# Scaling the values instead of the keys, and summing the first states on TensorE, in a retention layer with a feed-forward layer

## The chip, the cores and the metric

The kernel runs on one core of one Trainium2 chip. The metric is the device time of one execution in microseconds; the median of three runs counts. A second figure is the span of one profiled execution, from its first instruction to its last, which is a little shorter than the device time of that execution.

## The reference

Eight batches of eight heads, 576 positions of 64 numbers each, go through retention: attention without a softmax, in which the score of a query and a key falls by a factor gamma of the head with each step between them. The result, 4608 tokens of 512 numbers, goes through a feed-forward layer of 2048 with an ELU between.

```python
scores = q @ k.T / sqrt(64)                 # per batch and head
gamma  = 1 - 2 ** (-5 - head)
ret    = where(i >= j, scores * gamma ** (i - j), 0)
x      = (ret @ v)                          # heads side by side: 4608 x 512
h      = x @ w_in                           # 512 x 2048
out    = where(h > 0, h, exp(min(h, 0)) - 1) @ w_out    # 2048 x 512
```

## The kernel before

**The decay as two factors.** gamma^(i-j) is gamma^i times gamma^-j. The kernel keeps two small tables, `gq` (with the scale) and `gk`, and multiplies each query by its entry of `gq` and each key by its entry of `gk` while casting to bfloat16. The mask then only has to zero the upper triangle.

**Chunks and states.** A sequence is cut into blocks of 256 positions (`T` = 0, 1) and a tail of 64. Within a block, positions attend to each other by scores and mask; what lies before them comes in by a state, the sum of key times value over all earlier positions, 64 by 64 for each head. The first three batches are cut finer, into *units*: one batch, one block, four of the eight heads (`w` = 0, 1). Units 0 and 1 are the first block of batch 0, units 2 and 3 its second block, units 4 and 5 the first block of batch 1, and so on to 11. A unit has two chunks `c`, which lie on partitions 0 to 63 and 64 to 127. Units 0 to 5 are called *early* (`EARLY`): their scores and states are groups of their own on TensorE (`early`); later units and items are joined in pairs (`stretch`).

**A unit's way.** SyncE loads its queries, keys and values as float32 (tiles `r`; for the first two blocks the values come after the keys, `VLATE`). In `prepare_unit` two multiplies (even and odd positions, `e`) make bfloat16 queries and two make keys, in a tile `st`; one cast makes the values, tile `vn`. Queries and keys are transposed, by TensorE and a copy (tile `T`) up to unit 4 and by a DMA from unit 5 on (`PE_TURN`). TensorE then makes the scores, VectorE masks them into `pt` (L913), TensorE makes the unit's state (`do_state`, matmuls `vn,st`), and at last its output: the state before it times the queries (`T,s`) and the masked scores times the values (`pt,vn`). The output is cast to `xt`, the input of the feed-forward layer.

**The states' sums.** `do_state` makes one sum for each chunk, from 64 partitions each; the eight matmuls of chunk 0 and the eight of chunk 1 are interleaved and lie on different rows of the array. `after_state_unit` copies the first sum from PSUM into a float32 tile `mid` or adds it to the last one there, and casts each running sum into a bfloat16 tile `s` that TensorE can use.

**The feed-forward layer.** `ffn1` makes 512 columns by a group of matmuls (tile `f` in PSUM; 8 matmuls for a block of 256 tokens), ScalarE the exponential `e`, ScalarE or VectorE a relu or `em`, VectorE the ELU `g`. `ffn2` multiplies `g` by `w_out`, and the result leaves through `ot`. The weights are loaded by nine DMAs that GpSimd issues (`wi0` to `wi4` for w_in, `wo0` to `wo3` for w_out), in the queue of GpSimd's own instructions.

**The order.** Every step is an operation of a plan (`Plan.run`), with a cost for each engine that may do it, a rank and, for some, an earliest time (`AT`, `RANKS`). The plan is run with these costs before anything is issued; it chooses engine, order and buffer, and each engine then carries out its own list in that order, waiting where an input is not there. Tiles come from fixed numbers of slots (`SLOTS`; "f" are the eight PSUM banks). A group that needs several banks reserves them through `gate`, which lets it wait while at least `SURE` second-layer groups are ready. Where the plan sees TensorE idle in the first 50 us, it puts in filler matmuls on zeros (L1219, or `zero` at L275), as many as the gap it computed has room for. `HOLD` keeps the loads of unit 4 back until w_out's second piece has landed (L399). All matmuls have line L275 in the profile, transposes L579.

Of the kernel before, what the change touches and what calls it, by code (L numbers as in the profile page):

```python
# [12 lines left out]
BF16 = mybir.dt.bfloat16  # L13
I32 = mybir.dt.int32
AF = mybir.ActivationFunctionType
ALU = mybir.AluOpType
# [19 lines left out]
class Plan:  # L36
# [170 lines left out]
JOINT = True  # L207
BD_ACT = 0.6
TWO, STEP = 2, 4
WI, WI1, LD = 1.3, 1.65, 0.84  # L210
MOST, MOSTU = 4, 3
BD_POOL = 0.46
# [10 lines left out]
APART = (4, 5)  # L223
HOLD = {"ldq4": "wo1"}
VLATE = (0, 1)
AT = {"wi0": 8.5, "wi1": 9.1, "wi2": 8.7, "wi3": 11.8, "wi4": 15.0, "wo0": 15.9, "wo1": 18.0, "wo2": 18.9, "wo3": 25.0}
RANKS = {}
FREE = ("f", "e", "em", "g", "ot")
SURE = 3
ATT = ((0, 0), (0, 1), (1, 0), (1, 1), (2, 0), (2, 1), (3, 0), (3, 1), (4, 0), (4, 1), "X",  # L230
       (5, 0), (5, 1), (6, 0), (6, 1), (7, 0), (7, 1), "Y")
FFN = tuple(((b, T),) for b in range(7) for T in range(2)) + (("X", "Y"), ((7, 0), (7, 1)))
# [1 line left out]
W_OUT = ((0, 1), (1, 2), (2, 3), (3, 4))  # L234

SLOTS = {
    "f": 8, "r": 8, "st": 4, "kv": 3, "T": 4, "pt": 2, "vn": 5, "s": 6, "mid": 6,
    "xt": 3, "g": 33, "e": 4, "em": 4, "ot": 6, "S": 5, "bd": 8, "be": 8,
}

# [2 lines left out]
def kernel(  # L243
# [92 lines left out]
    def T(cls, key, shape, dt):  # L336
        return (cls, key, shape, dt)
# [198 lines left out]
    def prepare_unit(u):  # L536
        n = u.n
        key, vkey, tkey = ("qkn", n), ("vn", n), ("qkT", n)
        hs, begun, cq = slice(4 * u.w, 4 * u.w + 4), {}, {}
        for i in range(2):  # L540
            for e in range(2):
                g = (gq, gk)[i][:, 2 * u.T + e, hs].rearrange("p (x y) -> p x y", y=2)
                g = g.unsqueeze(3).to_broadcast([P, 2, 2, D])

                def emit(op, i=i, e=e, g=g):
                    raw = tiles["rqk", n].rearrange("p (h e) d -> p h e d", e=2)[:, 4 * i : 4 * i + 4, e]
                    pin(alu[op.eng].tensor_tensor(tiles[key][:, i, e].rearrange("p (y x) d -> p x y d", y=2),  # L547
                                                  raw.rearrange("p (x y) d -> p x y d", y=2), g, ALU.mult))

                kw, use = taking(begun, "st", key, [P, 2, 2, 4, D])  # L550
                cq[i, e] = add(f"c{'qk'[i]}{e}{n}", {"POOL": 0.62, "DVE": 0.5} if n < 4 else {"POOL": 0.64, "DVE": (0.6, 1.5)},
                               [u.ld["qk"[i]]], emit, u.rank, use=[("rqk", n), *use], **kw)
                begun.setdefault(key, cq[i, e])
        u.ck = [cq[1, 0], cq[1, 1]]

        def emit_v(op):
            pin(copy[op.eng](tiles[vkey], tiles["rv", u.it.n].rearrange("p (h e) d -> p h e d", e=2)[:, hs]))  # L557

        u.laid = [add(f"cv{n}", {"ACT": 0.62, "POOL": 0.65, "DVE": (0.42, 0.3)} if n < 4 else {"POOL": 0.65, "ACT": (0.62, 1.0)},
                      [u.ld["v"]], emit_v, u.rank, take=[T("vn", vkey, [P, 4, 2, D], BF16)], use=[("rv", u.it.n)])]  # L560
        u.cv = u.laid[0]

        def flat():
            return tiles[key].rearrange("p i e h d -> p (i e h d)")

        if n >= PE_TURN:
            def emit_t(op):
                pin(nc.sync.dma_start_transpose(tiles[tkey], flat()))

            u.turned = [add(f"tr{n}", {"SP": 1.23}, list(cq.values()), emit_t, -1, take=[T("T", tkey, [P, 8, P], BF16)],  # L570
                            use=[key], dma=(1.7, 64))]
            return
        u.turned = []
        for i in range(2):
            bkey = ("T", n, i)

            def emit_t(op, i=i, bkey=bkey):
                for j in range(4):
                    pin(nc.tensor.transpose(tiles[bkey][:, j], flat()[:, (4 * i + j) * P : (4 * i + j + 1) * P], ident))  # L579

            t = add(f"T{n}_{i}", {"PE": 0.35}, [cq[i, 0], cq[i, 1]], emit_t, u.rank - 4, take=[T("f", bkey, [P, 4, P], BF16)],
                    use=[key])

            def emit_c(op, i=i, bkey=bkey):
                pin(copy[op.eng](tiles[tkey][:, 4 * i : 4 * i + 4], tiles[bkey]))

            kw, use = taking(begun, "T", tkey, [P, 8, P])
            u.turned.append(add(f"cp{n}_{i}", {"DVE": 0.42, "ACT": 0.59}, [t], emit_c, u.rank - 4, use=[bkey, *use],
                                banks=[(bkey, 0)], **kw))
            begun.setdefault(tkey, u.turned[0])  # L590
# [180 lines left out]
    def do_state(it, tkey, off, st):  # L771
        if it.unit:
            kn, vn = tiles["qkn", it.n], tiles["vn", it.n]
            for b in range(2):
                for e in range(2):
                    for c in range(2):
                        for d in range(2):
                            to = (tkey, c if off == 0 else 1 - c)
                            st.put(c, d, to, tiles[to][rows(d), off + b * D : off + (b + 1) * D],
                                   kn[rows(c), 1, e, 2 * b + d], vn[rows(c), 2 * d + b, e])  # L780
            return
        kv = tiles["kv", it.n].rearrange("p m (h d) -> p m h d", h=H)
        for s in range(2):
            for z in range(2):
                for b in range(2):
                    for par in range(2):
                        for d in range(2):
                            st.put(par, d, (tkey, par), quad((tkey, par), s, 2 * b + z, rows(d)),
                                   kv[rows(par), KS[s], 4 * b + 2 * z + d], kv[rows(par), VS[s], 4 * z + 2 * d + b])
# [43 lines left out]
    def after_state_unit(u, st, tkey, off):  # L833
        for c in range(2):
            cc = 2 * u.T + c + 1
            bank, skey = (tkey, c if off == 0 else 1 - c), ("us", u.b, cc, u.w)
            prev = total.get((u.b, u.w))

            def st_ap(bank=bank):
                return tiles[bank][:, off : off + P].rearrange("p (h d) -> p h d", h=2)  # L840
# [24 lines left out]
            def emit_b(op, skey=skey, bkey=bkey):  # L865
                pin(copy[op.eng](tiles[bkey], tiles[skey]))

            bd_op.setdefault(bkey, []).append(
                add(f"ub{u.n}_{c}", {"POOL": UB_POOL, "ACT": (0.3, 0.3), "DVE": (0.2, 0.4 if u.early else 1.5)}, [s_op], emit_b,
                    u.rank + 3, take=[T("s", bkey, [P, 2, D], BF16)], use=[skey]))  # L870

    def after_state(it, st, tkey, off):
        if it.unit:
# [123 lines left out]
    def stretch(prev, it):  # L997
# [4 lines left out]
            use += inter_uses(prev)  # L1002
            cost += cost_of(prev, "iv") + (0.23 if it is None else 0)
        if it is not None:
            deps += [*it.turned, *([it.cv] if it.unit else [] if it.tail else it.laid)]
            use += [turned_of(it)] + ([] if not it.unit and it.tail else inputs_of(it))
            cost += cost_of(it, "s" if not it.unit and it.tail else "st")
        state = it is not None and (it.unit or not it.tail)
# [16 lines left out]
    def early(it):  # L1025
# [3 lines left out]
        mask_step(it, sc)  # L1029
        if it.unit or not it.tail:  # L1030
            tkey = ("t", it)
            st = add(f"st{name}", {"PE": cost_of(it, "t") + 0.17}, [*it.ck, it.cv] if it.unit else it.laid,
                     lambda op: alone(do_state, it, tkey, 0), it.rank + 1, use=inputs_of(it))
            reserve(st, pair_of(tkey))
            after_state(it, st, tkey, 0)
# [222 lines left out]
```

## Time and profile before

| | us |
|---|---|
| median of 3 runs | 299.97 |
| lowest and highest | 299.42, 300.76 |
| profiled execution, device time | 299.04 |
| its span | 297.3 |
| TensorE busy | 291.7 (98%) |
| VectorE busy | 201.7 (68%) |
| ScalarE busy | 160.3 (54%) |
| GpSimd busy | 118.6 (40%) |

In the profile PE is TensorE, PEld its loads of weights, DVE VectorE, ACT ScalarE, POOL GpSimd and SP SyncE. A row of a timeline gives the start in us, the length, the engine, the line, the operation, what it writes and reads, the shape and the count; in square brackets the idle time before it and what ended it. The clock that the profile grants TensorE is at its full value throughout. What is said of TensorE's being busy has to be read with care: filler matmuls count as busy too.

### The profile page before, as it was taken

To read this page: it belongs to the slowest core of one execution; us is meant where nothing else is said; L and a number is where in the kernel's file an instruction comes from. 1 tells how busy PE (TensorE), PEld (TensorE's weight loads), DVE (VectorE), ACT (ScalarE), POOL (GpSimd) and SP (SyncE) were. 2 spreads that over 40 slices of the span, in tenths; PEclk is the share of its full clock that TensorE was granted. 3 is DMA by queue.
4 is the path that set the end of the run, shared out by engine and by line. 5 is a ranking of instruction groups with operands and counts; after the bars stand their busy time and mean duration, and the time that the engine had idled before them with its cause. 6 is when DMAs were issued, how large, how long until landed. Compare 5 with 4: busy or idle time off the path is not lost.

```text
span 297.3 us, 9176 instructions
## 1 busy us (share of the span) xinstructions
PE 291.7 (98%) x3819; PEld 188.5 (63%) x3819; DVE 201.7 (68%) x385; ACT 160.3 (54%) x298; POOL 118.6 (40%) x193
## 2 busy tenths in 40 slices
PE   7999999999999999999999999999999999999995
PEld 4778556776665766677667676767666444444444
DVE  4979644878765867677787777767877567766500
ACT  3578514876633755466556466464565548644311
POOL 5980288394727361557447356370820000000000
PEclk9999999999999999999999999999999999999999
DMA  7999999999989994699989599987451100011221
GB/s 201 289 207 207 274 264 271 296 232 253 204 210 202 265 194 119 162 252 200 277 207 214 130 227 212 255 151 174 125 109 37 37 35 35 0 37 35 49 96 71
DMA packets 124554, 50.67 MB, mean 170 GB/s; under 512 B 84448, under 2 KB 120032, under 8 KB 124512
## 3 DMA queue, kind: packets, MB, share of 16 engines
q1 hardware_dynamic: 119760, 45.89, 66.3%
q0 software_dynamic: 4752, 4.19, 8.8%
q8 instruction: 30, 0.49, 0.7%
q14 instruction: 12, 0.10, 0.1%
HBM read 36.70 MB, written 9.44 MB: 155 GB/s over the span
## 4 chain that ended last, share of the span: by engine, by line
PE 94%; POOL 2%; DMA 2%; SPq 1%; issue 0%; ACT 0%; ACTq 0%
PE f L275 94%; DMA r<-in_v_dram 2%; POOL w_in_sb L479 1%; SPq L388 1%; POOL vn L557 0%; PE f L579 0%; POOL st L547 0%; ACT ot L1127 0%; PE f L1219 0%; ACTq L1127 0%
## 5 line engine op out<-in xcount | busy, mean ns | idle before, releaser
L275 PE MATMUL f<-w_out_sb,g 128*128 128x512 bf16 (+1 forms) x592 | 141.6, 374 | 0.0
L275 PE MATMUL f<-xt,w_in_sb 128*128 128x256 bf16 (+1 forms) x1024 | 141.1, 286 | 0.0
L1066 ACT ACTIVATE e<-f 128x512 f32<-128x512 f32 x144 | 85.5, 598 | 79.4 <-PE f L275 76.9
L275 PEld LDWEIGHTS <-w_in_sb 128*128 128x128 bf16 x1024 | 99.3, 98 | 38.6
L275 PEld LDWEIGHTS <-g 128*128 128x128 bf16 x592 | 56.6, 98 | 49.7
L1080 DVE TENSOR_SCALAR em<-e 128x512 bf16<-128x512 f32 x87 | 43.2, 496 | 40.6 <-ACT e L1066 40.4
L1090 DVE SCALAR_TENSOR_TENSOR g<-f,em 128x512 bf16<-128x512 f32 x87 | 59.3, 689 | 5.9
L1088 DVE SCALAR_TENSOR_TENSOR g<-e,f 128x512 bf16<-128x512 f32 x57 | 38.1, 683 | 11.3 <-ACT f L1076 10.2
L1127 ACT COPY ot<-f 128x512 f32<-128x512 f32 (+1 forms) x37 | 21.2, 574 | 22.5 <-PE f L275 22.1
L604 POOL CAST kv<-r 128x512 bf16<-128x512 f32 x24 | 14.3, 619 | 47.2 <-PE f L275 37.6
L624 POOL TENSOR_TENSOR kv<-r,gq 128x512 bf16<-128x512 f32 x24 | 25.7, 1091 | 15.4 <-DMA r<-in_q_dram 15.4
L1076 ACT ACTIVATE f<-f 128x512 f32<-128x512 f32 x52 | 30.7, 597 | 0.0
L949 ACT CAST xt<-f 128x512 bf16<-128x512 f32 (+1 forms) x39 | 21.5, 605 | 13.5 <-PE f L275 13.3
L624 POOL TENSOR_TENSOR kv<-r,gk 128x512 bf16<-128x512 f32 x24 | 25.3, 1056 | 3.9 <-DMA r<-in_k_dram 3.9
L913 DVE TENSOR_TENSOR pt<-f,mask_u 128x512 bf16<-128x512 f32 x24 | 15.4, 683 | 3.2 <-PE f L275 3.1
L917 DVE TENSOR_TENSOR pt<-f,mask 128x512 bf16<-128x512 f32 x24 | 15.3, 681 | 2.1 <-PE f L275 2.1
L902 POOL CAST bd<-S 128x256 bf16<-128x256 f32 x34 | 13.1, 408 | 4.6 <-ACT S L888 2.2
L547 POOL TENSOR_TENSOR st<-r,gq 128x256 bf16<-128x256 f32 x19 | 11.9, 645 | 6.6 <-DMA r<-in_q_dram 6.6
L890 DVE TENSOR_TENSOR S<-f,S 128x256 f32<-128x256 f32 x30 | 12.6, 421 | 2.1
L547 POOL TENSOR_TENSOR st<-r,gk 128x256 bf16<-128x256 f32 x19 | 11.9, 642 | 1.8 <-DMA r<-in_k_dram 1.6
L275 PE MATMUL f<-T 64*64 64x64 bf16 (+1 forms) x576 | 10.4, 202 | 0.0
L275 PEld LDWEIGHTS <-kv 64*64 64x64 bf16 x704 | 9.2, 104 | 0.0
(65 smaller groups left out, 138.0 us busy)
## 6 DMA issues: line engine op xcount, KB each, us to landing
r<-in_k_dram SPq DMA_DIRECT2D x32, 256.0 KB, 4.4
r<-in_v_dram SPq DMA_DIRECT2D x32, 256.0 KB, 4.8
out_dram<-ot SPq DMA_DIRECT2D x31, 256.0 KB, 2.9
r<-in_q_dram SPq DMA_DIRECT2D x10, 512.0 KB, 5.4
r<-in_q_dram SPq DMA_DIRECT2D x12, 256.0 KB, 4.5
w_out_sb<-in_moe_w_out_dram POOLq DMA_DIRECT2D x4, 512.0 KB, 13.2
w_in_sb<-in_moe_w_in_dram POOLq DMA_DIRECT2D x3, 512.0 KB, 8.8
out_dram<-ot SPq DMA_DIRECT2D x10, 128.0 KB, 2.3
```

The costliest lines, as they stand in the source:

```text
L275: return pin(nc.tensor.matmul(*a, **kw))
L547: pin(alu[op.eng].tensor_tensor(tiles[key][:, i, e].rearrange("p (y x) d -> p x y d", y=2), raw.rearrange("p (x y) d -> p x y d", y=2), g, ...
L624: pin(alu[op.eng].tensor_tensor(tiles[nkey][:, 2 * i + j].rearrange("p (y x d) -> p x y d", y=2, x=HP), raw.rearrange("p (x y) d -> p x y ...
L913: pin(nc.vector.tensor_tensor(pt, src.rearrange("p (h n) -> p h n", h=2), mask_u.rearrange("p k e r -> p (k e r)").unsqueeze(1).to_broadca ...
L917: pin(nc.vector.tensor_tensor(pt.rearrange("p h s n -> p (h s) n"), src.rearrange("p (h n) -> p h n", n=C), mask.rearrange("p e r -> p (e ...
L949: pin(copy[op.eng](dst, src))
L1066: pin(nc.scalar.activation(tiles[ekey], tiles[hkey], AF.Exp))
L1076: pin(nc.scalar.activation(ph, ph, AF.Relu))
L1080: pin(alu[op.eng].tensor_scalar_add(em, e, -1.0))
L1088: pin(nc.vector.scalar_tensor_tensor(g, e, -1.0, ph, ALU.add, ALU.min))
L1090: pin(nc.vector.scalar_tensor_tensor(g, ph, 0.0, tiles[mkey], ALU.max, ALU.min))
L1127: pin(copy[op.eng](tiles[okey][:, :width], tiles[pkey][:, :width]))
```

## The change

The decay of the keys moves to the values. It enters the result as a product of key and value in both places where they meet (scores times values, and the states), so it may stand on either. Keys are now cast plainly (`kk0`, `kk1`, on any of three engines), values are multiplied by `gk` in two halves of two heads each (`vs0`, `vs1`, on GpSimd or VectorE). For early units the state of the second chunk is made as one sum over both chunks, from all 128 partitions; the float32 running sum then takes only this one, and the state after the first chunk is cast (or added and cast) from PSUM straight into its bfloat16 tile (`early_state`). Slots for `s` go from six to eight, `SURE` from three to two, and due times and ranks of some steps are altered.

```diff
+KK = {"ACT": 0.37, "POOL": 0.38, "DVE": (0.26, 0.3)}
+VV = {"POOL": 0.62, "DVE": 0.5}
...
-AT = {"wi0": 8.5, "wi1": 9.1, "wi2": 8.7, "wi3": 11.8, "wi4": 15.0, "wo0": 15.9, "wo1": 18.0, "wo2": 18.9, "wo3": 25.0}
-RANKS = {}
+AT = {"wi0": 8.5, "wi1": 9.1, "wi2": 8.4, "wi3": 12.1, "wi4": 13.6, "wo0": 13.9, "wo1": 18.0, "wo2": 19.3, "wo3": 25.0, "kk1_1": 6.92, "T1_0": 6.8, "md_0_5": 32.14}
+RANKS = {"g_0_0": -8, "wo1": -2, "cq03": 8, "F1_0_0": -2}
...
-SURE = 3
+SURE = 2
...
-    "f": 8, "r": 8, "st": 4, "kv": 3, "T": 4, "pt": 2, "vn": 5, "s": 6, "mid": 6,
+    "f": 8, "r": 8, "st": 4, "kv": 3, "T": 4, "pt": 2, "vn": 5, "s": 8, "mid": 6,
...
     def prepare_unit(u):
...
+        for e in range(2):
+            def emit_k(op, e=e):
+                pin(copy[op.eng](natural(1, e), raw(1, e)))
...
+            cast[1].append(add(f"kk{e}_{n}", KK if n < 4 else
+                               {"POOL": 0.38, "ACT": (0.37, 0.8), "DVE": (0.26, 1.5)},
+                               [u.ld["k"]], emit_k, u.rank, use=[("rqk", n), *use], **kw))
...
-        def emit_v(op):
-            pin(copy[op.eng](tiles[vkey], tiles["rv", u.it.n].rearrange("p (h e) d -> p h e d", e=2)[:, hs]))
-
-        u.laid = [add(f"cv{n}", {"ACT": 0.62, "POOL": 0.65, "DVE": (0.42, 0.3)} if n < 4 else {"POOL": 0.65, "ACT": (0.62, 1.0)},
-                      [u.ld["v"]], emit_v, u.rank, take=[T("vn", vkey, [P, 4, 2, D], BF16)], use=[("rv", u.it.n)])]
+        for x in range(2):
...
+            def emit_v(op, x=x, g=g):
+                src = tiles["rv", u.it.n].rearrange("p (h e) d -> p h e d", e=2)[:, hs][:, 2 * x : 2 * x + 2]
+                pin(alu[op.eng].tensor_tensor(tiles[vkey][:, 2 * x : 2 * x + 2], src, g, ALU.mult))
...
+            u.laid.append(add(f"vs{x}_{n}", VV if n < 4 else {"POOL": 0.64, "DVE": (0.6, 1.5)},
+                              [u.ld["v"]], emit_v, u.rank, use=[("rv", u.it.n), *use], **kw))
...
     def do_state(it, tkey, off, st):
         if it.unit:
             kn, vn = tiles["qkn", it.n], tiles["vn", it.n]
+            if it.early:
+                for c in range(2):
+                    for b in range(2):
+                        for e in range(2):
+                            for d in range(2):
+                                own = slice(0, (c + 1) * C)
+                                acc((tkey, c), d, tiles[tkey, c][rows(d), off + b * D : off + (b + 1) * D],
+                                    kn[own, 1, e, 2 * b + d], vn[own, 2 * d + b, e])
+                return
...
+            if u.early and c == 0:
+                early_state(u, st, bank, cc, prev)
+                continue
...
+    def early_state(u, st, bank, cc, prev):
+        bkey = ("s", u.b, cc, u.w)
+
+        def emit(op):
+            src = tiles[bank][:, :P].rearrange("p (h d) -> p h d", h=2)
+            if prev is None:
+                pin(copy[op.eng](tiles[bkey], src))
+            else:
+                pin(nc.vector.tensor_tensor(tiles[bkey], src, tiles[prev[1]], ALU.add))
```

## The prediction

> **What bounds the kernel now.** I read the page first, then busy time by stretch, then TensorE's timeline up to 46 us, then the three other engines up to 42 us. The page says that TensorE is busy nearly throughout, at the full granted clock (tenths, 9 is the highest digit):
>
> ```profile
> PE 291.7 (98%) x3819; PEld 188.5 (63%) x3819; DVE 201.7 (68%) x385; ACT 160.3 (54%) x298; POOL 118.6 (40%) x193
> ...
> PEclk9999999999999999999999999999999999999999
> ```
>
> A busy TensorE may still be running fillers, so I cut the span at 19.77 us, where the feed-forward layer begins to run without a break. Columns: length, then busy us and instructions of PE, PEld, DVE, ACT, POOL, then clock and DMA:
>
> ```profile
> 0.00:19.77 19.77, 17.42 (x341) 12.41 (x342) 14.24 (x46) 10.35 (x23) 15.50 (x33) 1.00 1.04 236
> 19.77:294.14 274.37, 274.27 (x3481) 176.08 (x3478) 187.50 (x340) 149.63 (x275) 103.13 (x161) 1.00 0.75 167
> 294.14:297.30 3.16, 0.00 (x0) 0.00 (x0) 0.00 (x0) 0.37 (x1) 0.00 (x0) 1.00 0.12 41
> ```
>
> From 19.77 to 294.14 us TensorE is busy 274.27 of 274.37 us. Nothing waits there that could be taken out: only a shorter list of matmuls, or an earlier start, moves the end. So the change is decided before 19.77 us, and by new gaps after it. TensorE's timeline shows how that start comes about (start, length of the group with its last drain, what, count):
>
> ```profile
> 9.34 0.29 PE L275 MATMUL f<-vn,st 64*64 64x64 bf16 x16
> ...
> 15.61 0.32 PE L275 MATMUL f<-vn,st 64*64 64x64 bf16 x16
> 15.86 1.05 PE L275 MATMUL f<-xt,w_in_sb 128*128 128x256 bf16 x8
> 16.84 0.42 PE L275 MATMUL f<-T 64*64 64x128 bf16 x16
> 17.09 0.23 PE L275 MATMUL f<-T,s 64*64 64x128 bf16 x4
> ...
> 17.85 1.05 PE L275 MATMUL f<-xt,w_in_sb 128*128 128x256 bf16 x8
> 18.83 0.25 PE L275 MATMUL f<-T,s 64*64 64x128 bf16 x4
> ...
> 19.59 0.34 PE L275 MATMUL f<-zero 128*128 128x128 bf16 x3
> 19.77 12.39 PE L275 MATMUL f<-xt,w_in_sb 128*128 128x256 bf16 x112
> ```
>
> Differences of start times give the price of each step: state of unit 3 0.25, a feed-forward group of 8 matmuls 0.98, scores 0.25, the rest of attention for one unit 0.76 (17.09 to 17.85, and 18.83 to 19.59), three fillers 0.18. The same sixteen state matmuls took 0.16 (9.34 to 9.50) where a matmul of the same tile shape followed: a change of tile shape costs 0.09. The last thing that this chain waits for is data: ScalarE casts the values of unit 3 as they land.
>
> ```profile
> 14.93 0.62 ACT L557 CAST vn<-r 128x512 bf16<-128x512 f32 x1 [1.09 <-DMA r<-in_v_dram]
> ```
>
> Two DMA issues later matter as well. GpSimd issues the weights between its conversions:
>
> ```profile
> 7.16 0.85 POOL L547 TENSOR_TENSOR st<-r,gk 128x256 bf16<-128x256 f32 x1
> ...
> 9.20 2.43 POOL L479 DMA_DIRECT2D w_in_sb<-in_moe_w_in_dram  x3
> ...
> 14.63 0.60 POOL L547 TENSOR_TENSOR st<-r,gk 128x256 bf16<-128x256 f32 x1
> ...
> 15.42 0.80 POOL L479 DMA_DIRECT2D w_in_sb<-in_moe_w_in_dram  x1
> 16.22 0.75 POOL L490 DMA_DIRECT2D w_out_sb<-in_moe_w_out_dram  x1
> ```
>
> The first of the three w_in pieces is issued at 9.20 and the DMA view puts its landing 6.1 us later, at 15.3; the first feed-forward group cannot start before. GpSimd's multiply takes 0.60 alone and 0.85 when VectorE multiplies at the same moment; a DMA issue costs it 0.75 to 0.94. VectorE's rows:
>
> ```profile
> 13.36 0.83 DVE L547 TENSOR_TENSOR st<-r,gk 128x256 bf16<-128x256 f32 x1
> ...
> 15.39 1.29 DVE L913 TENSOR_TENSOR pt<-f,mask_u 128x512 bf16<-128x512 f32 x2
> ```
>
> Its multiply was 0.42 alone (next one 0.34 later), 0.83 for the slower of these two beside GpSimd; a mask is 0.64 (0.60 to the next).
>
> **The change part by part.** *Keys cast, values scaled.* Per unit, two key multiplies become two casts of 128x256, and one cast of 128x512 becomes two multiplies. On GpSimd after 35 us two multiplies take 1.15 from start to start and the cast 0.57, together 2.85 a unit. A cast of 128x256 lies between the 0.29 of 128x128 and the 0.60 of 128x512; the bd cast of that size has a mean of 0.41, and I take 0.37: 1.15 + 0.74 + 1.15 = 3.04, 0.2 more (0 to 0.5). GpSimd is 40% busy, and this is hidden as long as unit 4 is in time: its queries land at 35.5, so its keys are ready at 35.54 + 1.15 + 0.74 = 37.4. The new order asks for them after 112 first-layer and 24 second-layer matmuls and the query transposes. From a start of 20.0 that is 20.0 + 12.23 + 24 x 0.216 + 0.22 = 37.6. In time by 0.2; without that cover the excess is paid one for one.
>
> *First 8 us.* Keys of unit 0 are cast on ScalarE and GpSimd at once instead of waiting for a 0.82 GpSimd multiply, so its scores move from 7.30 to about 7.0. This gain does not last: unit 1 needs data that lands at 7.1 (keys) and 8.6 (values), then 16 fillers follow, and its values part comes out at 11.2 as before.
>
> *Values of unit 3 on VectorE.* This adds a wait. Before, ScalarE took these values alone. Now VectorE's half stands in its queue ahead of the first mask of unit 2, the copy of unit 3's transposes, the second mask and the state sums. The data lands at 14.92: VectorE 14.93, next at 15.28, mask to 15.88, copy to 16.30, and with the 0.12 from a copy's end to the matmul (8.97 to 9.09) scores of unit 3 can start at 16.42. TensorE comes there by itself at 15.4 (w_in landed) + 0.98 + one filler = 16.45. So the wait is just covered by the first feed-forward group; later by x, all behind it is later by x.
>
> *Values of unit 3 on GpSimd.* The other half stands behind two weight issues. From 8.69 (unit 0's second half, 0.85): 0.60 for unit 1, to 9.29; issues 0.94 + 0.75 + 0.75; query multiply 0.67; state cast 0.25; issue 0.81; key cast 0.37; values of unit 2 0.70; issues 0.81 + 0.75; this half 0.60: 16.7. The state of unit 3 asks for it at 16.45 + 0.25 = 16.70. No slack. The w_out issues behind it are early: the first hold on a w_out landing is seen at 29.6.
>
> *State in one sum.* The matmul count stays sixteen a unit; eight now use all 128 rows. No 128-row matmul of 64 columns is in the trace. Lower end 0: count and columns are the same. Upper end: transposes of 128x128 start 0.055 apart, 8 x 0.055 against 8 x 0.010, plus one shape change, 0.36 + 0.09 = 0.45. The nearest row is the sixteen in 0.16, so I take a low value, 0.10 a unit. It counts for unit 3 on the path and units 4 and 5 in the full stretch; units 0 to 2 have fillers or waits beside them. The Trainium skill, TensorE: Matmul & The Clock Gate, Part 3 (packing small matmuls), speaks against this edit: matmuls run at the same time where they lie on different row groups of the array, and its summary says that one on a few rows takes as long alone as one on all. By it the eight lose their partners by rows; an estimate from its section on the back-to-back issue gap (columns at 2.4 GHz plus 2.5 ns) is 8 x 0.029 less 0.08 us, 0.15 a unit, and the sum would be 0.15 us above mine.
>
> *First state straight from PSUM.* One copy less per early unit (0.27 on ScalarE or VectorE) and no float32 copy for the first chunk. Off the chain: the sums of units 2 and 3 are wanted at 18.0 and 19.2 and are done by 17.3 and 18.8.
>
> *Due times, ranks, SURE, slots.* They only move the order. In the built order of the full stretch, the number of first- and second-layer matmuls, of attention matmuls and of tile-shape changes (48) is unchanged.
>
> *The new start.* Scores of unit 3 at 16.45, +0.25, state +0.35, second feed-forward group +0.98, unit 2 +0.76, six fillers 6 x 0.056 + 0.09 = 0.43, unit 3 +0.76: 19.98 against 19.77. The state now stands after the first group instead of before it; the three extra fillers are lost time.
>
> **The sum.** Start +0.21, units 4 and 5 +0.20: +0.4 us. The span becomes 297.7; the profiled execution 299.04 becomes 299.4. That execution is 0.93 below the median of the runs, 299.97, so the median becomes 300.4 us, 0.14% slower.
>
> **The rivals.** *GpSimd late (slower).* If the conversions and issues cost what the dearest rows show (four multiplies 0.85 each, +0.8; five issues 0.94, +0.8), the values of unit 3 come at 18.3 and not 16.7. From 16.70 on each us is one at the end; past 17.8 the change is over half a per cent. Time 300.4 + 1.6 = 302.0. For it: no slack, and 0.85 and 0.94 both occur. Against: the dear multiplies stood beside VectorE's own from SBUF, and near 16 us it masks from PSUM. Chance 0.15. The Trainium skill, SBUF — State Buffer, section "Who interferes with whom", makes this a lock: of a VectorE instruction with two SBUF inputs and a GpSimd instruction that reads SBUF, the later one waits until the other is through. By it a multiply that starts with VectorE's would take 0.60 + 0.42; the trace shows 0.85, and by the page the chain above would end about 0.2 later.
>
> *No loss.* If the full-row matmuls are free and nothing waits at 16.45, w_in's landing leaves 15.4 + 0.98 + 0.25 + 0.25 + 0.98 + 0.76 + 0.43 + 0.76 = 19.8: time 300.0. For it: all terms are rows; against: no slack anywhere. Chance 0.20.
>
> *Dear state matmuls.* 0.45 a unit for units 3, 4, 5: +1.05, time 301.4. Chance 0.10.
>
> *Faster by over 0.5%.* It would need 1.5 us out of a stretch with 0.1 us of idle time, or a first layer that starts before its weights allow. No row gives it; 0.05 for what I don't see.
>
> **How the numbers follow.** Forecast 0.50, no loss 0.20, dear matmuls 0.10, GpSimd late 0.15, faster 0.05. Half a per cent, 1.5 us, is about what a measurement of this kernel can tell from no change (its three runs span 1.34 us). Within it lie the first three but for 0.01 at the dear end: 0.79; slower 0.16; faster 0.05. The range goes from the case of no loss less half that spread, 299.3, to the dear matmuls plus 0.4 of it, 301.8; it leaves out the faster case and nearly all of GpSimd late, under 0.2.
>
> **What would show it.** Right: VectorE waits for the values' DMA just before 14.9 us; unbroken first-layer matmuls from 20.0 (19.9 to 20.4); no wait of TensorE after that; last matmul at 294.5. Wrong: TensorE waiting on GpSimd's values near 16.7 for over 1 us; a gap near 37.5 before the key transposes of unit 4; state matmuls over 0.3 us a unit; or the first layer running unbroken before 19.5.

## The result, and the profile after

Over 22 executions of each kernel the changed one takes 300.96 us in the median (299.98 to 302.27), the one before 299.80 (298.82 to 303.78): 1.0046 times as long, 95% interval 1.0036 to 1.0056. The forecast was 300.4 us, 0.14% slower, inside the half per cent that counts as no change. It came out 0.46% slower, at the upper edge of that: 1.16 us between the medians, where 0.43 were forecast. The profiled execution took 300.98 us, with a span of 299.3.

The page of the changed kernel, TensorE and its clock:

```profile
PE 290.1 (97%) x3779; PEld 189.2 (63%) x3817; DVE 200.1 (67%) x378; ACT 162.4 (54%) x303; POOL 119.1 (40%) x201
...
PEclk9999999999999999999999999999999999999999
```

Nothing has changed here: TensorE is the bound, at a granted clock of 0.999. Busy time by stretch, cut again where the first layer begins to run without a break (here 21.17 us) and where the last copy of ScalarE begins (columns: stretch, length, busy us and instructions of PE, PEld, DVE, ACT, POOL, clock, DMA share, GB/s):

```profile
0.00:21.17 21.17, 18.21 (x341) 12.92 (x342) 14.13 (x44) 10.86 (x25) 15.29 (x38) 1.00 1.01 224
21.17:296.10 274.93, 271.84 (x3444) 176.25 (x3476) 185.92 (x335) 151.13 (x277) 103.85 (x163) 1.00 0.76 167
296.10:299.30 3.20, 0.00 (x0) 0.00 (x0) 0.00 (x0) 0.37 (x1) 0.00 (x0) 0.93 0.12 41
```

Of the 2.0 us that the two profiled spans lie apart, 1.40 stand in the start (21.17 against 19.77) and 0.56 in the unbroken stretch (274.93 against 274.37). The busy time of the long stretch looks 3 us short: it has 3444 matmul records against 3476 loads of weights, so 32 are missing from the trace. TensorE's timeline of the start (start, length, what, count, idle time before it and what ended it):

```profile
11.24 0.32 PE L277 MATMUL f<-vn,st 128*64 128x64 bf16 x8
11.49 1.07 PE L277 MATMUL f<-zero 128*128 128x128 bf16 x16
...
15.07 0.59 PE L277 MATMUL f<-vn,st 64*64 64x64 bf16 x16
15.59 0.40 PE L600 MATMUL f<-ident,st 128*128 128x128 bf16 x4
...
16.45 1.05 PE L277 MATMUL f<-xt,w_in_sb 128*128 128x256 bf16 x8 [0.35 <-DMA w_in_sb<-in_moe_w_in_dram]
17.33 0.22 PE L277 MATMUL f<-zero 128*128 128x128 bf16 x1
17.51 0.42 PE L277 MATMUL f<-T 64*64 64x128 bf16 x16
17.76 0.53 PE L277 MATMUL f<-vn,st 64*64 64x64 bf16 x16
18.22 1.05 PE L277 MATMUL f<-xt,w_in_sb 128*128 128x256 bf16 x8
...
19.96 0.51 PE L277 MATMUL f<-zero 128*128 128x128 bf16 x6
...
21.17 12.40 PE L277 MATMUL f<-xt,w_in_sb 128*128 128x256 bf16 x112
```

The order is the forecast one: first feed-forward group, one filler, scores, state and second group, and six fillers before unit 3's output. Two things differ. The state of a unit takes 0.52 (15.07 to 15.59, unit 2) and 0.46 (17.76 to 18.22, unit 3) where it took 0.25 before; 0.06 of the 0.52 are a wait of its second matmul for GpSimd's half of the values, done at 15.07. And the first group waits 0.35 us for w_in, which landed late in this execution. The first row shows eight state matmuls with the new shape, over all 128 partitions; rows of sixteen hold eight of each shape under the name of the first.

The values of unit 3, on VectorE and on GpSimd:

```profile
16.10 0.43 DVE L577 TENSOR_TENSOR vn<-r,gk 128x256 bf16<-128x256 f32 x1 [0.73 <-DMA r<-in_v_dram]
16.44 0.68 DVE L960 TENSOR_TENSOR pt<-f,mask_u 128x512 bf16<-128x512 f32 x1
```

```profile
15.81 0.75 POOL L492 DMA_DIRECT2D w_out_sb<-in_moe_w_out_dram  x1
16.57 0.64 POOL L577 TENSOR_TENSOR vn<-r,gk 128x256 bf16<-128x256 f32 x1
```

VectorE waits for the load, with the mask behind it, as forecast. GpSimd's half is done at 17.2, and TensorE comes to the state at 17.76.

### The profile page after: what moved, and what is told of

It reads as the page before. It is cut to its first block, busy times and chain, and to the rows that moved or that the text cites. A ratio compares the mean times of both kernels' runs of the same rounds, so it can differ in the third digit from the quotient of the medians.

```text
span 299.3 us, 9140 instructions
## 1 busy us (share of the span) xinstructions
PE 290.1 (97%) x3779; PEld 189.2 (63%) x3817; DVE 200.1 (67%) x378; ACT 162.4 (54%) x303; POOL 119.1 (40%) x201
## 4 chain that ended last, share of the span: by engine, by line
PE 92%; DMA 4%; issue 1%; SPq 1%; POOL 0%; ACT 0%; ACTq 0%; POOLq 0%
PE f L277 92%; DMA w_in_sb<-in_moe_w_in_dram 2%; DMA r<-in_v_dram 2%; SPq L390 1%; POOL vn L577 0%; PE f L600 0%; ACT ot L1174 0%; ACTq L1174 0%; POOLq L577 0%
## 5 line engine op out<-in xcount | busy, mean ns | idle before, releaser
L277 PE MATMUL f<-w_out_sb,g 128*128 128x512 bf16 (+1 forms) x556 | 137.2, 373 | 2.7 <-issue 1.4
L1137 DVE SCALAR_TENSOR_TENSOR g<-f,em 128x512 bf16<-128x512 f32 x88 | 60.2, 689 | 6.3 <-DVE em L1127 0.5
L996 ACT CAST xt<-f 128x512 bf16<-128x512 f32 (+1 forms) x42 | 22.8, 601 | 14.8 <-PE f L277 14.6
L1123 ACT ACTIVATE f<-f 128x512 f32<-128x512 f32 x51 | 30.0, 595 | 0.0
L577 POOL TENSOR_TENSOR vn<-r,gk 128x256 bf16<-128x256 f32 x20 | 12.5, 642 | 1.8 <-DMA r<-in_v_dram 1.8
```

What stands on the lines that cost most here:

```text
L277: return pin(nc.tensor.matmul(*a, **kw))
L996: pin(copy[op.eng](dst, src))
L1123: pin(nc.scalar.activation(ph, ph, AF.Relu))
L1137: pin(nc.vector.scalar_tensor_tensor(g, ph, 0.0, tiles[mkey], ALU.max, ALU.min))
```

## The experiments

Each kernel was timed beside the kernel before on the same chip; its medians there were 299.47, 299.51, 299.40 and 299.46 in the four series. The text names the theories in words, since the letters of the expectations were not used alike in all series. Before_again is a single execution (300.10 us) and has no row.

| kernel | median us (lowest to highest) | ratio to before, 95% |
|---|---|---|
| half_rows | 299.76 (299.28 to 300.60) | 1.0007 [0.9992, 1.0022] |
| one_sum_only | 300.35 (299.29 to 302.15) | 1.0023 [1.0002, 1.0043] |
| old_times | 301.05 (299.91 to 303.56) | 1.0053 [1.0031, 1.0074] |
| after_again | 300.66 (300.23 to 301.72) | 1.0031 [1.0012, 1.0050] |
| all_rows | 300.70 (299.94 to 302.54) | 1.0044 [1.0024, 1.0065] |
| after_nofill | 300.82 (299.38 to 302.67) | 1.0036 [1.0014, 1.0057] |
| before_nofill | 300.53 (298.81 to 303.96) | 1.0028 [1.0000, 1.0056] |
| two_sums | 304.10 (300.53 to 304.68) | 1.0138 [1.0098, 1.0177] |
| wi0_early | 301.45 (300.06 to 305.70) | 1.0079 [1.0044, 1.0113] |
| decay_only | 302.91 (300.69 to 306.31) | 1.0111 [1.0071, 1.0151] |
| two_sums_nofill | 300.41 (299.12 to 301.73) | 1.0035 [1.0016, 1.0054] |

### The state matmuls back on their own rows: half_rows

```diff
     def do_state(it, tkey, off, st):
         if it.unit:
-            if it.early:
-                for c in range(2):
...
-                return
```

> The changed kernel, in the same order on every engine, but the state of an early unit's second chunk is summed over its own 64 rows alone, so the eight matmuls of 128 rows become eight of 64 and interleave with the other eight as before (left out: the first chunk's part of that sum). Theory A (128-row matmuls are dearer than I took, 0.2 us a unit and more): the state group of units 4 and 5 goes back from about 0.48 us (start to next start) to 0.25, that of unit 3 from 0.46 to 0.25 or 0.16; the stretch from the unbroken start to the last matmul goes back from 274.96 to about 274.4 us, and the time falls by 0.5 to 0.8 us against the changed kernel. Theory B (their price is the 0.10 of the prediction, the rest is elsewhere): time falls by 0.3 us or less.

This is the cleanest pair: the order of all engines is that of the changed kernel, and only these matmuls differ. Half_rows is 0.90 us faster than after_again beside it by the medians, 0.7 by the ratios; 0.5 to 0.8 were expected if the matmuls of 128 rows are dear. Its timeline:

```profile
16.39 0.29 PE L277 MATMUL f<-vn,st 64*64 64x64 bf16 x16
16.72 1.03 PE L277 MATMUL f<-xt,w_in_sb 128*128 128x256 bf16 x8
...
19.65 3.12 PE L277 MATMUL f<-xt,w_in_sb 128*128 128x256 bf16 x27
...
42.50 0.32 PE L277 MATMUL f<-vn,st 64*64 64x64 bf16 x16
42.75 2.76 PE L277 MATMUL f<-w_out_sb,g 128*128 128x512 bf16 x11
```

The cleanest place for the price is unit 5, the last two rows: nothing waits there, and the same kinds of matmul stand ahead of the state and behind it in both kernels. The changed kernel, in its first profile:

```profile
44.26 0.56 PE L277 MATMUL f<-vn,st 64*64 64x64 bf16 x16
44.75 2.76 PE L277 MATMUL f<-w_out_sb,g 128*128 128x512 bf16 x11
```

From start to next start the state takes 0.49 there and 0.25 in half_rows: 0.24 a unit. Unit 4 gives 0.24 too (0.69 and 0.45, from 40.24 to 40.93 and from 38.72 to 39.17, with a matmul record behind it missing in both). The state of unit 3 is down to 0.33 from 0.46, and the unbroken start is at 19.65. From there to the last matmul 274.4 us were expected and 274.7 measured, against 274.9 in the first profile of the changed kernel: the 0.48 of units 4 and 5 is there at 45 us, and 0.3 of it is lost again from 65 us on.

The ratio to the kernel before is 1.0007 with 1 inside the interval: with the states' matmuls as they were, the rest of the change, in this order, can't be told from nothing (at most 0.7 us by the interval).

### The other half alone: one_sum_only

To the kernel before, the block in `do_state`, `early_state` and eight slots for `s` were added, and the plan's cost of a state group rises by 0.06 as in the changed kernel; keys, values, due times and ranks stayed. The plan orders the steps anew.

```diff
+            if it.early:
+                for c in range(2):
...
+                                own = slice(0, (c + 1) * C)
...
+            if u.early and c == 0:
+                early_state(u, st, bank, cc, prev)
+                continue
```

> The kernel before with the second part of the change alone: one sum over both chunks for early units, first state cast straight from PSUM, eight slots for s; keys still scaled, due times as before. Theory A (the matmuls of 128 rows carry about half of the loss): slower than before by 0.4 to 0.8 us. Theory B (the loss comes from keys and values, that is from GpSimd and VectorE before the weights are issued): within 0.3 us of before.

It is 0.88 us slower than the kernel before by the medians, 0.7 by the ratio (0.1 to 1.3 by its interval), and its groups cost the same as in the changed kernel (15.98 to 16.47, 0.49):

```profile
15.98 0.56 PE L275 MATMUL f<-vn,st 64*64 64x64 bf16 x16 [0.49 <-ACT vn L557]
16.47 1.05 PE L275 MATMUL f<-xt,w_in_sb 128*128 128x256 bf16 x8
```

So the sum over 128 partitions costs some 0.7 to 0.9 us when it is added alone, with all that goes with it, and its matmuls give about as much back when they are taken away alone. Each of the two sizes is uncertain by half a microsecond.

### All sixteen over 128 rows: all_rows

```diff
-                                own = slice(0, (c + 1) * C)
+                                own = slice(0, P)
```

> The changed kernel in the same order, but all sixteen state matmuls of an early unit use all 128 rows (changed: the first chunk's state then holds the second chunk too). It tells apart what the 128-row matmuls cost: the tile-shape change in the middle of a group (0.09) or the lost sharing of the array by rows. If the change of shape is the larger part: the group of units 4 and 5 takes about 0.40 us from its start to the next start, against 0.48, and the time falls a little (0 to 0.3 us). If the lost sharing is: each further 128-row matmul costs 0.03 against 0.010, the group takes 0.55 or more, and the time rises by 0.2 to 0.5 us.

```profile
16.65 0.42 PE L277 MATMUL f<-T 64*64 64x128 bf16 x16
17.00 0.44 PE L277 MATMUL f<-vn,st 128*64 128x64 bf16 x16
17.37 1.05 PE L277 MATMUL f<-xt,w_in_sb 128*128 128x256 bf16 x8
...
43.94 0.44 PE L277 MATMUL f<-vn,st 128*64 128x64 bf16 x16
44.32 1.90 PE L277 MATMUL f<-w_out_sb,g 128*128 128x512 bf16 x8
```

More work per matmul, and the group is shorter: 0.37 against 0.46 to 0.52. Together with the starts of single matmuls in the traces this takes the price apart. In the kernel before, they start four at a time, within 0.010 us, and about 0.03 us lie from one four to the next: two row halves and two column halves of the array work at once. Sixteen are four such rounds. In the changed kernel they come two at a time, also about 0.03 apart: the eight of chunk 0 have no partners on the other rows, and the eight that use all rows leave none free. That is eight rounds instead of four, +0.13. Between the two shapes one step takes 0.123 instead of 0.032, +0.09. Together 0.22, with 0.24 measured. At unit 5 all_rows has the eight rounds but not the change of shape in the middle: 0.25 + 0.13 = 0.38, measured 0.38. The Trainium skill, TensorE: Matmul & The Clock Gate, Part 3, says that matmuls overlap where their row groups differ; the trace agrees with it. By the section on the back-to-back issue gap, on the same page of the Trainium skill, a round would be 0.029; the trace has 0.028 to 0.032.

Yet all_rows is no faster than after_again by its median, and its rows say why little was to be gained. The change of shape has not gone; ahead of units 2, 3 and 4 it has moved in front of the group. The scores of unit 3 now take 0.35 (16.65 to 17.00) where they took 0.25, so scores and state together take 0.72, as in the changed kernel (0.71, from 17.51 to 18.22). Only unit 5, which has no 64x64 matmuls just ahead of it, is 0.11 shorter. Neither half of the expectation is borne out: the group became shorter, as the change of shape alone would have it, but the lost sharing costs as much (0.13 against 0.11), and the time did not move. The two medians are of different chips, so a tenth of a microsecond can't be read from them.

### Due times and ranks: old_times, and the kernels again: after_again, before_again

```diff
-AT = {..., "wi2": 8.4, "wi3": 12.1, "wi4": 13.6, "wo0": 13.9, ..., "kk1_1": 6.92, "T1_0": 6.8, "md_0_5": 32.14}
-RANKS = {"g_0_0": -8, "wo1": -2, "cq03": 8, "F1_0_0": -2}
-SURE = 2
+AT = {..., "wi2": 8.7, "wi3": 11.8, "wi4": 15.0, "wo0": 15.9, ...}
+RANKS = {}
+SURE = 3
```

> The changed kernel with the due times, ranks and SURE of the kernel before. Theory A (only the 128-row matmuls and the later weights cost time, whatever the due times): within 0.4 us of the changed kernel. Theory C (the altered due times and ranks, with six fillers between the last two outputs of attention, cost it): faster than the changed kernel by 0.5 us or more.

> The changed kernel once more, for a second profile. Theory D (the loads of the first 5 us land at other times in each execution): the third load, issued at 1.85, lands at another time than 6.83 us, somewhere between 6.0 and 7.0, and the first w_in piece and the unbroken start move with it. Theory E (the change itself makes the loads land later): it lands at 6.8 again, 0.7 after that of the kernel before.

> The kernel before once more, for a second profile. Theory D (loads land at other times in each execution): its third load lands at another time than 6.11 us and the unbroken start moves with it, by up to 0.7 us. Theory E (loads land early in this kernel always): third load within 0.1 of 6.11 us, unbroken start within 0.1 of 19.77.

Old_times is 0.39 us above after_again by the medians, with overlapping intervals; its profiled execution holds a wait of 3.21 us at 155 us, of which more below. It is within the 0.4 us of the first theory and not faster, but with that wait in it the run settles little. What clears the due times is half_rows, which has the altered ones and is as fast as the kernel before.

The two repetitions show how far one execution can mislead. After_again:

```profile
15.49 1.04 PE L277 MATMUL f<-xt,w_in_sb 128*128 128x256 bf16 x8
...
16.76 0.59 PE L277 MATMUL f<-vn,st 64*64 64x64 bf16 x16
17.28 1.05 PE L277 MATMUL f<-xt,w_in_sb 128*128 128x256 bf16 x8
...
20.22 2.47 PE L277 MATMUL f<-xt,w_in_sb 128*128 128x256 bf16 x21
```

Before_again:

```profile
19.66 0.34 PE L275 MATMUL f<-zero 128*128 128x128 bf16 x3
20.67 2.03 PE L275 MATMUL f<-xt,w_in_sb 128*128 128x256 bf16 x17 [0.67 <-DMA w_in_sb<-in_moe_w_in_dram]
```

The same two kernels, and now the changed one starts at 20.22 and the one before at 20.67. The loads land differently from one execution to the next. The third piece of w_in is issued at 10.87 and 10.93 in the two of the kernel before, and lands at 19.16 and 20.62. In the two of the changed kernel the values of unit 3 take 6.79 and 5.08 us from issue to landing (16.07 and 13.71), and the first piece of w_in, issued 0.66 apart behind conversions that wait for loads, lands at 16.41 and 14.97. The start of the changed kernel moves by 0.95 us with this. As for the load that the expectations named, the third one: in the changed kernel it moved (GpSimd's multiply that waits for it starts at 6.97 and at 6.36), in the kernel before it did not (6.11 and 6.10), and the start moved all the same, with the third piece of w_in. A comparison of one profile with one profile can't carry a difference of 1 us here; the medians have to.

### The fillers: after_nofill and before_nofill

Fillers are put in before 12 us only, not before 50.

```diff
-            gap = op.start - last if op.start < 50 and last else 0.0
+            gap = op.start - last if op.start < 12 and last else 0.0
```

> The changed kernel without the fillers that the plan puts in from 12 us on (seven before a transposition, then 1, 2, 1 and six). Theory: the six between the last two attention outputs are lost time, 0.34 and a shape change, so the distance from the second feed-forward group's start to the unbroken start falls from 2.95 to about 2.5 us, and the time falls by 0.3 to 0.5 us. Rival: without them TensorE waits just as long for the masks or for data (distance unchanged), or its clock is held lower (clock below 1.0).

> The kernel before without the fillers from 12 us on (among them three ahead of the unbroken start and two near 49 us with two shape changes). Theory: 0.18 at the start and 0.25 near 49 us, together 0.3 to 0.5 us faster than before, which would make it the fastest so far. Rival: TensorE waits instead, no difference.

The six fillers were counted as 0.43 us lost. From the second feed-forward group to the unbroken start it is 2.41 us without them and 2.94 with them, so they do cost that. But the time did not fall (300.82). In its profile part of the gain goes to a wait inside the state of unit 3, which takes 0.70 instead of 0.46: its second matmul comes 0.24 after the first, once GpSimd's half of the values is done at 17.17. Without the fillers TensorE gets there 0.2 us before GpSimd is done.

```profile
16.53 0.64 POOL L577 TENSOR_TENSOR vn<-r,gk 128x256 bf16<-128x256 f32 x1
```

```profile
16.98 0.77 PE L277 MATMUL f<-vn,st 64*64 64x64 bf16 x16
17.68 1.05 PE L277 MATMUL f<-xt,w_in_sb 128*128 128x256 bf16 x8
```

The rest is given back at a transposing DMA of a later unit:

```profile
66.10 0.22 PE L277 MATMUL f<-T,s 64*64 64x128 bf16 x2
66.93 0.42 PE L277 MATMUL f<-T 64*64 64x128 bf16 x16 [0.61 <-DMA T<-st]
```

The kernel before without its fillers loses its clock. Its clock row, and its first feed-forward group:

```profile
PEclk9979999999999999999999999999999999999999
```

```profile
16.30 1.89 PE L275 MATMUL f<-xt,w_in_sb 128*128 128x256 bf16 x8
```

The group takes 1.89 instead of 1.05: in this kernel the fillers keep the clock up. Its five executions at full clock (0.998 or more) have a median of 299.56 us, no faster than the kernel before (299.51), so the 0.3 to 0.5 us expected from the fillers did not come either way. The changed kernel without them kept its clock in 11 of 12 executions, the kernel before in 5 of 12; their work around 14 us is spread differently, and TensorE's longest wait there is 0.6 against 1.0 us.

### A version with both sums and the plain keys: two_sums, decay_only, two_sums_nofill

Half_rows leaves a part of the second state out. These kernels leave nothing out: keys cast, values multiplied, states as before (two_sums), and the keys and values part alone on the tables of the kernel before (decay_only). In both the plan's cost of a state group goes back with the states, and the plan orders the steps anew.

```diff
 # two_sums, against the changed kernel: the early blocks of do_state and after_state_unit out
-            if it.early:
...
-            if u.early and c == 0:
-                early_state(u, st, bank, cc, prev)
-                continue
 # decay_only: the same, and AT, RANKS, SURE and the slots of the kernel before
```

> The changed kernel with the whole state part put back as it was (two sums of 64 partitions, interleaved, running sum in float32 from both chunks); keys stay cast plainly and values multiplied. Unlike half_rows it gives the reference's output, but the plan orders the steps anew, because the copies of the first sums are back. Theory A (the 128-row state matmuls cost 0.24 us a unit and carry about 0.9 of the 1.2 us lost): state groups back at 0.25 us, median 299.6 to 300.0, ratio to before 1.000 to 1.002. Theory B (the loss is in keys and values, and half_rows was fast because it left work out): median 300.5 or more, ratio over 1.003. If moving the decay were worth anything by itself, the ratio would be under 0.999.

> The kernel before with the keys and values part of the change alone: keys cast plainly, values multiplied by gk in halves; states, slots, due times, ranks and SURE as in the kernel before. It is the counterpart of one_sum_only. Theory A (the sum over 128 rows carries the loss): state groups 0.25 us, median 299.5 to 300.2 and ratio 1.000 to 1.002, provided TensorE has no long wait for nothing that the profile shows. Theory B (keys and values carry it): ratio over 1.003 with no such wait. Theory C, from the profiles of two_sums and old_times (2.38 and 3.21 us without any instruction at 155 us, where a packet of the instruction queue moves): this order too may load TensorE's instructions late; then the time is 2 to 4 us up in those executions, with the wait at about 155 us in the profile, and says nothing about A or B until the wait is taken off.

Both lose 3 to 5 us, and the states are not the cause (unit 3 of two_sums: 17.34 to 17.57, 0.23). The expectation of two_sums did not have this; that of decay_only, written after it, did. TensorE stands still in the middle of the full stretch and waits for nothing that the profile shows. Two_sums, old_times and decay_only, in that order:

```profile
157.38 0.39 PE L277 MATMUL f<-xt,w_in_sb 128*128 128x256 bf16 x2 [2.38 <-issue]
```

```profile
158.35 0.27 PE L277 MATMUL f<-xt,w_in_sb 128*128 128x256 bf16 x1 [3.21 <-issue]
```

```profile
156.88 0.28 PE L277 MATMUL f<-xt,w_in_sb 128*128 128x256 bf16 x1 [1.46 <-issue]
```

In each of the three, one 16 KB packet of the instruction queue moves just before: it ends at 155.93, 156.93 and 155.44, and TensorE goes on 1.45, 1.42 and 1.44 us later. The pause also comes at the same place of TensorE's list, behind 2268, 2266 and 2268 weight loads, though not at the same time. Both point to one cause, which the profile does not show directly: TensorE's next instructions had not been loaded. In two_sums the pause costs more than itself. Its busy time by stretch (length, busy us and count of PE, clock, DMA share, GB/s):

```profile
155.00:157.38 2.38, 0.01 (x2) 1.00 0.66 126
157.38:159.00 1.62, 1.62 (x10) 0.89 1.23 256
159.00:161.00 2.00, 2.00 (x9) 0.50 1.21 266
161.00:163.00 2.00, 2.00 (x13) 0.74 0.06 14
```

The clock is halved for some 3.4 us after it, another 1.62 x 0.11 + 2 x 0.50 + 2 x 0.26 = 1.7 us: 4.1 in all. The Trainium skill, TensorE: Matmul & The Clock Gate, Part 1, has the clock fall after an idle window of about 3.4 us. Here 2.38 us were enough, and in old_times 3.21 us were not: its clock stays at 1.00.

```diff
 # two_sums_nofill, against two_sums: no fillers from 12 us on
-            gap = op.start - last if op.start < 50 and last else 0.0
+            gap = op.start - last if op.start < 12 and last else 0.0
```

> two_sums without the fillers after 12 us: about 40 instructions fewer in TensorE's list ahead of 155 us. Two_sums had 2.38 us without any instruction at 155.00 and then half the granted clock to 162 us, 4.1 us together. Theory C (the loading of TensorE's instructions comes late where a block of 256 ends inside a dense stretch of short matmuls): the ends of the blocks move by some 40 instructions, the wait at 155 us goes or changes by over 1 us, and the median falls to 299.8 to 301. Rival (the wait belongs to the work at that place, such as a load that lands late): it stays within 0.5 us of 2.4, median 303.5 or more. For Theory A: with the wait off, 299.6 to 300.4.

The fillers that went were 24, not the 40 expected. That was enough: the wait at 155 us is gone (the longest wait of this kind is 0.16 us) and the median falls by 3.7 us, to 300.41, as the theory of late instructions expected. For the two theories about the change it decides nothing: 300.41 is 1.0035 times the kernel before, and in its profile the clock fell near 16 us instead, as in before_nofill. So no version here beats the kernel before.

What the keys and values cost by themselves is settled only for the order of the changed kernel, by half_rows: 0.2 us, not to be told from 0. In other orders it stays open. In two_sums the 302.6 us of the span less 4.1 make 298.5, and in decay_only 300.3 less 1.46 make 298.8, where the kernel before had 297.3 and 298.4. In the orders that the plan makes there, a third feed-forward group and eight or eleven fillers come ahead of the unbroken stretch. Those are one profile each, and their 0.1 to 1.5 us above the kernel before lie within the scatter of the loads.

### An earlier load of w_in: wi0_early

```diff
-AT = {"wi0": 8.5, ...
+AT = {"wi0": 8.0, ...
```

> The kernel before with one number altered: the earliest time of the first w_in load 8.0 instead of 8.5. It asks whether the start of the first layer hangs on the landing of w_in. If it does (the first feed-forward group starts within 0.6 us behind w_in's first landing in all profiles), an issue earlier by up to 0.5 us gives a median lower by 0.2 to 0.5 us, ratio 0.998 to 0.999, and the unbroken stretch from about 19.3. If the landing is set by what the DMA queues still have to move, or if the third piece or the values of unit 3 come last, the ratio is 1.000 within 0.0015.

The first piece is issued at 7.93 instead of 9.20 and lands at 14.04 instead of 15.25. The first group starts at 15.41, only 0.45 earlier. The values of unit 3, which move at the same time on the same 16 DMA engines, land at 18.12 instead of 14.90, and the unbroken stretch begins only at 22.46, with two more groups already done. The kernel is 1.0079 [1.0044, 1.0113] times as long; neither expectation had a loss. The profiled execution is one of its fastest (300.25), so what the others lost is not seen. The plan also orders the start anew for the altered time (unit 3's state now stands behind the third group), so this is not the load alone. Still, an earlier load was not an earlier start here: another one landed later.

## Why the prediction came out as it did

**The bound.** Right: TensorE's list of matmuls, its start and its length, decide. What else held TensorE up after the first group is small: 0.06 us (GpSimd's half) and 0.23 us (a transposing DMA) are the largest such waits in after_again. That the time lies inside the range is owed to the range's width: the loss is nearly three times the one that the sum gave.

**The start.** The chain held, step by step. From the first feed-forward group to the unbroken start 4.58 us were forecast; 4.72 (after) and 4.73 (after_again) were measured. The missing 0.15 are nearly all in the state of unit 3, 0.46 and 0.52 instead of 0.35. The start itself was forecast at 19.98 and came at 21.17 and 20.22: above the range of 19.9 to 20.4 once, inside once. The first time the landing of w_in, taken as a fixed 15.3, was 16.41; the second time it was 14.97, and the state of unit 2 came last (below).

**The state in one sum.** Here the sum went wrong. The term was 0.10 a unit; it measures 0.24 (0.25 and 0.49 at unit 5). The nearest row (sixteen in 0.16) was read as one price per matmul, and not as four rounds of four that run at once; and the change of tile shape, priced at 0.09 on the same page of the prediction, was not counted inside the group. The prediction says that the full stretch keeps its 48 changes of tile shape; the trace of the kernel before has 48, that of the changed kernel 50, one more in each of units 4 and 5. The estimate by the Trainium skill, 0.15, was nearer, and with that 0.09 it would have been 0.24; it counted the eight one by one, though, where the trace shows them in pairs, so that the agreement is partly luck. The mark "state matmuls over 0.3 us a unit" was not clear: as an added cost 0.24 stays below it, as the length of the group 0.46 to 0.52 is over it, and about this step that reading was the true one.

**Which units count.** Units 3, 4 and 5 were counted. Unit 2 counts too: in after_again w_in had landed at 14.97, and the first group started at 15.49, behind unit 2's state (14.63 to 15.15), four transposes and two fillers. Unit 1's output, told for 11.2 "as before", came at 11.83 there, but what followed waited 0.40 us for a conversion at 14.11 anyway. With 0.24 for units 2 to 5 the sum, worked out afterwards, is 0.21 + 0.14 + 0.24 for the start and 0.48 for units 4 and 5: 1.07 us, against 1.16 between the medians and 1.1 to 1.7 by the interval of the ratio.

**VectorE and GpSimd.** The wait on VectorE came as told in the first profile (0.73 us, mask behind it) and was covered by the first group. In after_again the values had landed at 13.71, and VectorE came to them only at 14.85: its query multiply of 13.70 took 1.23 us instead of 0.42, while GpSimd cast and multiplied from 13.64 to 14.63. In the first profile, too, a multiply of VectorE that began during one of GpSimd's ended 0.30 after it (15.37 and 15.07). So one seems to wait for the other, as the rival "GpSimd late" has it, only here it was VectorE that waited. "GpSimd late" did not happen at its size. In after_again, where the loads land as early as forecast, the half ends at 16.77 and TensorE comes to the state at 16.76: forecast were 16.7 and 16.70. The second matmul of the state waits for it until 16.82, 0.06 us; in after_nofill the same wait is 0.24. "No slack" was right. Unit 4 was in time: there is no gap ahead of its key transposes (38.59).

**No loss, dear matmuls.** "No loss" fell with the full-row matmuls not being free. "Dear state matmuls" had the mechanism, at 0.45 a unit nearly twice the measured price; the truth lies between it and the forecast, 0.6 above the one and 0.4 below the other (300.4, 300.96, 301.4).

**No wait after the start.** Nearly right. After_again waits 0.23 us for a transposing DMA at 66.69, and after_nofill 0.61: an earlier start meets the conversions of later units. "Last matmul at 294.5" follows the start and failed with it.

## What to carry to other kernels

Price small matmuls by rounds that run at once, not by count: a sum over all 128 rows saves an addition elsewhere but takes away the row partner of every matmul in it, and a new tile shape adds a change of shape, inside the group or in front of it. In a chain, count a dearer step for every unit whose cover is a load of uncertain landing. Before trusting a difference of 1 us between two profiles, profile each kernel twice, and look first at waits for which the profile names no cause: they may belong to a place in the list of instructions and not to the change.

## What the runs showed of the hardware

- TensorE can stand still in the middle of a dense stretch with no cause in the profile: 1.46, 2.38 and 3.21 us at about 155 us in three kernels, behind 2266 to 2268 weight loads, ended 1.42 to 1.45 us after a packet of the instruction queue. The likely cause is that its next instructions were not there yet. Leaving 24 fillers out made it go. The times of two_sums vary from 300.53 to 304.68 us; whether the pause is in all of them is not shown. Why that packet is late is open.
- The time from a load's issue to its landing varies between executions: 7.99 to 9.69 us for the third piece of w_in, 5.08 to 6.79 for the values of unit 3, in two profiles of each kernel.
- Matmuls of 64 columns start four at a time on 64x64 tiles and two at a time on 128x64 tiles, about 0.03 us from one round to the next. A change of tile shape costs 0.09 us within a group of state matmuls too, as between groups.
- After the pause of 2.38 us (two_sums) the clock was halved for some 3.4 us; after one of 3.21 us (old_times) it was not.
